# Wider warm-up matmuls, tile 2 in two token parts, and the last semaphore waits ahead of the last store

## The chip, the cores and the metric

The kernel runs on one core of a Trainium2 chip. The metric is device microseconds (us) of one execution. The kernel before takes 579.82 us as the median of 10 runs (579.07 to 580.83). A profile was taken of one execution of 579.62 us, whose span on the core is 577.9 us.

Engine names as in the profile: PE is TensorE's matmuls, PEld its weight loads, DVE is VectorE, ACT is ScalarE, POOL is GpSimd, and SP is SyncE, which here only issues DMAs and waits.

## The reference

Inputs are bfloat16; S = 2048 tokens, D = 576 features, F = 4608 hidden features, 32 heads of 18.

```python
xn = layernorm(x)                                   # no scale, no shift
q, k, v = split(xn @ wqkv)                          # 32 heads of 18
scores = q @ k.T * 18 ** -0.5                       # key at most 255 tokens back, never ahead
s = (softmax(scores) @ v) @ wo
h = sigmoid(xn @ w_gate) * (xn @ w_up)
g = silu(h @ w_down)
out = x + s * g
```

So one normalized input feeds two branches, a sliding-window attention and a gated feed-forward network, whose results are multiplied.

## The kernel before

Tokens are worked in 4 chunks of 512, each of 4 blocks of 128. For each chunk: layer norm on DVE (with a power on POOL for the reciprocal root), a transposed copy `xnT` with features on partitions, projections of v, q and k, attention for 8 groups of 4 heads, the output projection, then the feed-forward network: 36 gate/up tiles of 128 hidden features over the chunk's 512 tokens, and the down projection, accumulated over all 36 tiles for each block of tokens. A final step multiplies the branches, adds x and stores the block.

576 is 4.5 times 128. So all large matmuls come in pairs that use 64 rows of the array each and run side by side (`pair`); 5 blocks of 128 contraction rows, one of them holding the first 64 features twice, make a whole product (`turn`). A gate/up tile is 5 pairs (`f10`, first half) and 4 pairs (`f11`, second half) of 512 columns; one member of the pair writes gate, the other up. This is why layer norm writes 640 columns: the first 64 are stored a second time (`ln:dup`), for chunk 0 by POOL from x itself, for later chunks by a DVE copy of what `ln:ap` wrote.

A gate/up tile occupies one of the PSUM slots of pool F (a slot is two banks; a third slot is shared with pool S, which serves everything else). ACT takes tanh of gate (L887), DVE multiplies it with up into `hT` (L890, `hm`), and then the slot is free. A scores matmul (`sc`) occupies a slot of pool S until ACT has taken its exponential (L701).

Nothing of the order on an engine is written by hand. `build_graph` makes a list of operations with dependencies, an engine, an estimated duration, and a priority. `schedule` plays them through with those estimates: among the operations that are ready it takes the earliest, each point of priority counting as 10 ns of delay, and so fixes each engine's instruction order and the PSUM slot of each tile. `emit` writes the five instruction streams, with a semaphore wait ahead of an instruction where it needs another engine's result; each engine then runs its stream in order. A DMA has a lane, a semaphore of its own kind; there are 58 lanes.

The beginning: the four blocks of chunk 0 are loaded by one DMA each, then the weights. While layer norm works on them, PE multiplies zeros (`warm`): 60 operations, each a pair of 256 columns, estimated at 220 ns for the first 18 and 110 ns for the rest, with low priority, so that `schedule` fits them where PE would stand. When the first gate/up matmul is placed, those left over are dropped; 45 are in the stream: 24, the transposes of block 0, 12, those of block 1, 9. The first three gate/up tiles of chunk 0 are begun before all tokens are there. Each is cut into parts by token blocks (`PARTS`: block 0, block 1, blocks 2 and 3), and `build_ffn` lists part by part, first halves of the three tiles, then second halves.

The end: PE's last matmuls are the down projection of the last block. ACT and DVE make the last columns, SP stores the block. After its last DMA, SP waits on every lane in turn, at most two lanes in one instruction (L1149 to L1151), and the kernel ends when all engines have met:

```python
            if e == "SP":
                for i, n in enumerate(lane_cnt):
                    if n > 0:
                        eng.wait_ge(lanes[i], n)
                eng.nop()
```

The softmax here doesn't subtract the row's maximum and nothing guards it: scores larger than these inputs give would overflow.

## Time and profile before

| what | us |
|---|---|
| median of 10 runs | 579.82 |
| lowest and highest | 579.07, 580.83 |
| the profiled execution | 579.62 |
| its span on the core | 577.9 |
| PE busy in it | 570.5 |
| DVE, ACT, POOL busy | 345.8, 267.8, 180.0 |
| first matmul of zeros | 1.15 |
| first matmul of real data | 9.10 |
| first gate/up matmul over all 512 tokens | 15.84 |
| last DVE sum begins | 574.45 |

How to read the lines. A timeline line gives the start in us, the time from the first start to the last end in us, engine, line, operation, the tile written and the tile read, and how many instructions of the kind are merged in it; in brackets stand the engine's idle time before it and what ended that. The start-to-start distance is the time that a matmul takes of PE; the time of a single one is longer, since matmuls are pipelined. PE's matmuls are counted one by one, so a pair is x2. A line of one source line gives the count, the duration in ns as minimum, median and maximum, and the first and the last start. A line of waits gives the total in us, the number and the longest. The chain's line gives each engine's share of the chain of work that ended last.

### The profile page before, as it was taken

Reading aid. Unit: us, or ns where it says so; the run is one execution under the profiler, and the core shown is the slowest. Engines: PE = TensorE matmul, PEld = TensorE weight load, DVE = VectorE, ACT = ScalarE, POOL = GpSimd, SP = SyncE. Lnnn points to the kernel's source line nnn. Section 1 sums busy time; section 2 is a strip of 40 time slices with the busy share of each in tenths; the row PEclk is TensorE's granted clock in tenths of the full one; section 3 lists DMA queues with packets and bytes.
Section 4 is the critical chain, followed back from the end, with each engine's and each line's share of the span. In section 5 each row is a group of like instructions: output and inputs, shape, how many; then the busy total and the mean of one; then the engine's idle time right before and its main releaser. Section 6 shows DMA issues by size and latency. Waiting matters only on the chain.

```text
span 577.9 us, 21485 instructions
## 1 busy us (share of the span) xinstructions
PE 570.5 (99%) x9542; PEld 361.7 (63%) x9542; DVE 345.8 (60%) x837; ACT 267.8 (46%) x379; POOL 180.0 (31%) x290
## 2 busy tenths in 40 slices
PE   9999999999999999999999999999999999999996
PEld 7455455678985556555788875555457754444786
DVE  4478889845899775577876578877321133333123
ACT  2257567421776653866663566685221023232111
POOL 7466454107564443145534354340000000000000
PEclk9999999999999999999999999999999999999999
DMA  8978865822313434233511023343440015442010
GB/s 248 265 201 206 230 185 165 200 46 55 89 51 108 120 98 116 83 92 103 110 36 43 19 63 103 105 117 111 116 141 23 23 58 154 133 137 74 2 43 23
DMA packets 104908, 62.06 MB, mean 107 GB/s; under 512 B 15308, under 2 KB 103452, under 8 KB 104816
## 3 DMA queue, kind: packets, MB, share of 16 engines
q1 hardware_dynamic: 99696, 55.95, 35.5%
q0 software_dynamic: 5120, 4.74, 3.3%
q8 instruction: 75, 1.23, 0.9%
q14 instruction: 17, 0.14, 0.1%
HBM read 51.61 MB, written 2.36 MB: 93 GB/s over the span
## 4 chain that ended last, share of the span: by engine, by line
PE 97%; DVE 2%; issue 1%; ACT 0%; DVEq 0%
PE ps L98 96%; DVE hT L890 1%; PE ps L550 1%; ACT tring L887 0%; DVE pvs L767 0%; DVE s_attn L994 0%; DVE thf L999 0%; DVE xf L1004 0%; DVE expr L714 0%; DVE pvs L771 0%; DVE hT L418 0%; DVE small L486 0%; DVE small L409 0%; ACT expr L701 0%; DVEq L1144 0%
## 5 line engine op out<-in xcount | busy, mean ns | idle before, releaser
L98 PE MATMUL ps<-xnT,wgs 64*128 64x512 bf16 (+2 forms) x2400 | 288.3, 368 | 0.1
L98 PEld LDWEIGHTS ps<-xnT,wgs 64*128 64x128 bf16 x2400 | 111.4, 94 | 113.9 <-PE ps L98 1.6
L701 ACT ACTIVATE expr<-ps 128x1024 bf16<-128x1024 f32 (+2 forms) x160 | 156.2, 983 | 52.2 <-PE ps L98 51.7
L98 PE MATMUL ps<-wd_sb,hT 64*128 64x288 bf16 (+2 forms) x2448 | 154.9, 276 | 0.0
L887 ACT ACTIVATE tring<-ps 128x512 bf16<-128x512 f32 x144 | 85.7, 596 | 129.6 <-PE ps L98 127.1
L890 DVE SCALAR_TENSOR_TENSOR hT<-tring,ps 128x512 bf16<-128x512 bf16 x144 | 98.6, 686 | 78.5 <-ACT tring L887 76.4
L98 PEld LDWEIGHTS ps<-wd_sb,hT 64*128 64x128 bf16 x2448 | 117.8, 94 | 22.5
L254 POOL DMA_DIRECT2D qk<-qd x160 | 82.3, 522 | 85.7 <-DVE qd L588 48.0
L666 POOL TENSOR_SCALAR kx<-kprev,small 128x256 bf16<-128x256 bf16 x64 | 64.8, 1022 | 72.0 <-PE ps L98 71.6
L714 DVE TENSOR_TENSOR expr<-expr,mask 128x256 bf16<-128x256 bf16 (+2 forms) x232 | 64.9, 301 | 29.8 <-ACT expr L701 28.4
L767 DVE TENSOR_REDUCE pvs<-ps 64x304 f32<-64x608 f32 x64 | 50.4, 788 | 17.5 <-PE ps L98 16.3
L98 PE MATMUL ps<-qk,kx 64*128 64x320 bf16 (+4 forms) x736 | 59.8, 251 | 0.0
L98 PE MATMUL ps<-xnT,wgr 64*128 64x512 bf16 (+2 forms) x300 | 55.8, 368 | 1.4 <-DVE hT L890 1.2
L98 PEld LDWEIGHTS ps<-qk,kx 64*128 64x128 bf16 x736 | 31.6, 94 | 25.4 <-ACT expr L701 1.7
L984 ACT ACTIVATE thf<-ps 128x576 bf16<-128x576 f32 (+3 forms) x22 | 11.4, 519 | 70.0 <-PE ps L98 69.5
L98 PEld LDWEIGHTS ps<-v_aug,expr 64*128 64x128 bf16 x2432 | 35.5, 93 | 6.2 <-issue 0.2
L98 PE MATMUL ps<-v_aug,expr 64*128 64x19 bf16 (+1 forms) x2432 | 35.8, 170 | 0.0
L98 PE MATMUL ps<-xnT,wqk 64*128 64x512 bf16 x256 | 32.0, 376 | 0.0
L588 DVE CAST qd<-ps 128x1024 bf16<-128x1024 f32 (+1 forms) x20 | 22.1, 1115 | 7.7 <-PE ps L98 7.5
L666 DVE TENSOR_SCALAR kx<-qk,small 128x512 bf16<-128x512 bf16 x64 | 23.7, 390 | 5.1 <-DMA qk<-qd 4.4
L987 DVE SCALAR_TENSOR_TENSOR thf<-thf,ps 128x576 bf16<-128x576 bf16 x12 | 9.1, 755 | 29.3 <-ACT thf L984 28.8
L670 POOL COPY kprev<-qk 128x256 bf16<-128x256 bf16 x32 | 13.5, 430 | 33.2 <-DVE kx L666 32.7
(66 smaller groups left out, 296.1 us busy)
## 6 DMA issues: line engine op xcount, KB each, us to landing
wgs<-in_B_w_gate_dram SPq DMA_DIRECT2D x72, 256.0 KB, 3.0
wgs<-in_B_w_up_dram SPq DMA_DIRECT2D x72, 256.0 KB, 3.5
wd_sb<-in_B_w_down_dram SPq DMA_DIRECT2D x9, 576.0 KB, 4.6
qk<-qd POOLq DMA_DIRECT2D x100, 36.0 KB, 2.0
xf<-in_A_x_dram SPq DMA_DIRECT2D x16, 144.0 KB, 2.5
out_dram<-xf SPq DMA_DIRECT2D x16, 144.0 KB, 1.8
xr<-in_A_x_dram SPq DMA_DIRECT2D x6, 288.0 KB, 3.7
wqk<-in_A_wqkv_dram SPq DMA_DIRECT2D x2, 576.0 KB, 6.2
```

What stands on the lines that cost most here:

```text
L98: res = eng.matmul(outs[i], lhs(ROWS[t], i), rhs(ROWS[t], i), start=start, stop=stop, tile_position=(64 * t, 0))
L254: o = self.op(eng, DMA_ISSUE_NS[eng], lambda e: e.dma_start(dst, src), name, deps, prio, nbytes=nbytes)
L588: return eng.tensor_copy(dst, self.both(h, n))
L666: return e.tensor_scalar(self.kx[:, sx, pos:pos + n_ // SW, t, :], src.rearrange("p (s k) -> p s k", k=SW), self.half[:, t:t + 1], None, A ...
L670: self.op_kp[hg] = op("POOL", 420, lambda e: e.tensor_copy(self.kprev[:, hg, :], self.qk[:, qs, 1, NT // 2:NT]), f"kp:{c}:{hg}", deps=[kxo ...
L701: return eng.activation(self.expr[:, se, :, lo * SW:NT], self.both(h, NT)[:, :, lo * SW:NT], ACTF.Exp, scale=SM_SCALE)
L714: return eng.tensor_tensor(e_, e_, m_, ALU.mult)
L767: return eng.tensor_reduce(out[ROWS[i]], src, mybir.AxisListType.X, ALU.add)
L887: th = op("ACT", act_ns(NT), lambda e: e.activation(self.tring[:, st, :], bank(h, 0), ACTF.Tanh, scale=0.5), f"th:{c}:{ft}", deps=[pg, dt_ ...
L890: mu = op("DVE", dve_ns(NT), lambda e: e.scalar_tensor_tensor(self.hT[:, ft, :], self.tring[:, st, :], 1.0, bank(h, 1), ALU.add, ALU.mult) ...
L984: return e.activation(v2(t)[:, a:b, :], y2()[:, a:b, :], ACTF.Tanh, scale=0.25)
L987: q1 = op("DVE", dve_ns(w), lambda e: e.scalar_tensor_tensor(v2(t), v2(t), 1.0, y2(), ALU.add, ALU.mult), f"fq1:{nm}", deps=[th, f2], prio=0)
```

## The change

There are four edits.

- The warm-up matmuls become 512 columns wide; there are up to 36, estimated at 432 ns for the first 9 and 216 ns for the rest. The zeros that they read are 512 columns, so the memset is twice as large.
- `PARTS` is given for each tile: tiles 0 and 1 as before, tile 2 in two parts (blocks 0 and 1, blocks 2 and 3). The list is made tile by tile, part by part, without the order of first and second halves over the tiles; `schedule` orders them by readiness.
- For chunk 0 too, the first 64 columns are stored a second time by a DVE copy after `ln:ap`.
- SP waits on all lanes but those of the output stores ahead of its last instruction, the last store; after it, on the store lanes only.

`XPRIO` is 0, so the priority of the loads of x is what it was. Since durations, engines and parts differ, `schedule` gives other orders throughout. In the built streams there are now 25 warm-up pairs (15, the transposes of block 0, 7, those of block 1, 3), and 9 pairs fewer in the first three tiles; DVE has four copies more and POOL four operations fewer; the counts of all other matmuls, of ACT's work and of DMAs are the same. In chunk 1, the first projection of q and k and the first scores stand earlier: the scores begin after the third group of down-projection matmuls of chunk 0's second block, not after the second group of its second half. PE's order from the end of chunk 3's attention on (beside tile 21 of chunk 2's gate/up tiles) is the same.

```diff
--- before.py
+++ after.py
@@ -53,8 +53,9 @@
 NQD = 2
 NFIN = 2
 NTAIL = 96
-NWARM = 60
-PARTS = ((0, 1), (1, 2), (2, 4))
+NWARM = 36
+PARTS = (((0, 1), (1, 2), (2, 4)), ((0, 1), (1, 2), (2, 4)), ((0, 2), (2, 4)))
+XPRIO = 0
 NQK = 5
 
 DMA_ISSUE_NS = {"SP": 640.0, "POOL": 520.0, "ACT": 650.0}
@@ -379,7 +380,7 @@
     def load_x(self, c, i=0):
         if c == 0:
             for i in range(BPC):
-                self.x_dma[i] = (self.dma(self.x0[:, i, :], self.x[i * P:(i + 1) * P, :], P * D * 2, f"dma:x{i}", ("x0", i), prio=0),
+                self.x_dma[i] = (self.dma(self.x0[:, i, :], self.x[i * P:(i + 1) * P, :], P * D * 2, f"dma:x{i}", ("x0", i), prio=XPRIO * (i > 1)),
                                  self.x0[:, i, :])
             return
         st = c * BPC + i
@@ -414,7 +415,7 @@
         self.op_ident = op("POOL", 200, lambda e: e.affine_select(
             self.ident[:, :], self.ident[:, :], pattern=[[1, SW]], compare_op=ALU.not_equal, fill=1.0, base=SW,
             channel_multiplier=-1), "init:ident3", deps=[o2], prio=0)
-        zero = self.hT[:, 0, 0:2 * P]
+        zero = self.hT[:, 0, :]
         z = op("DVE", 600, lambda e: e.memset(zero, 0.0), "init:zero", prio=0)
         self.op_tab = op("ACT", 1500, lambda e: e.activation(self.tring[:, 0, 0:1], zero[:, 0:1], ACTF.Exp), "init:tab",
                          deps=[z], prio=0)
@@ -422,8 +423,8 @@
         w = None
         for i in range(NWARM):
             def f_warm(eng):
-                return pair(eng, self.halves(h, 2 * P), lambda r, t: zero[r, 0:P], lambda r, t: zero[r, :], True, True)
-            w = op("PE", 220 if i < 18 else 110, f_warm, f"warm:{i}", deps=[z], prio=4, acq=None if i else h, odeps=[w])
+                return pair(eng, self.halves(h, NT), lambda r, t: zero[r, 0:P], lambda r, t: zero[r, :], True, True)
+            w = op("PE", 432 if i < 9 else 216, f_warm, f"warm:{i}", deps=[z], prio=4, acq=None if i else h, odeps=[w])
             w.filler = h
             h.release(w)
 
@@ -493,17 +494,11 @@
             ap = op("DVE", 430, lambda e, ss=ss, x_in=x_in, sn=sn: e.tensor_scalar(
                 self.xnr[:, sn, RD:XW], x_in, self.mv[:, ss, 0:1], self.rstd[:, ss, :],
                 ALU.subtract, ALU.mult), f"ln:ap:{st}", deps=[rs, ag, dn], prio=pr)
-            if c:
-                dup = op("DVE", 180, lambda e, sn=sn: e.tensor_copy(self.xnr[:, sn, 0:RD], self.xnr[:, sn, RD:2 * RD]),
-                         f"ln:dup:{st}", deps=[ap], prio=pr)
-            else:
-                dup = op("POOL", 260, lambda e, ss=ss, x_in=x_in, sn=sn: e.tensor_scalar(
-                    self.xnr[:, sn, 0:RD], x_in[:, 0:RD], self.mv[:, ss, 0:1], self.rstd[:, ss, :],
-                    ALU.subtract, ALU.mult), f"ln:dup:{st}", deps=[rs, ag, dn], prio=pr)
+            dup = op("DVE", 180, lambda e, sn=sn: e.tensor_copy(self.xnr[:, sn, 0:RD], self.xnr[:, sn, RD:2 * RD]),
+                     f"ln:dup:{st}", deps=[ap], prio=pr)
             if c:
                 self.r_xr.release(i % 2, ap)
             self.r_st.release(ss, ap)
-            self.r_st.release(ss, dup)
             if c:
                 fl = self.flip(self.xnT[:, xs, :, i * P:(i + 1) * P], self.xnr[:, sn, :], f"flip:x:{st}", ("fx", xs, i),
                                deps=[dup, war], prio=2)
@@ -867,7 +862,7 @@
 
         def gate_up(ft, h, half, acq, part=None, deps=()):
             sw, fc = slots[ft // WG], slice((ft % WG) * P, (ft % WG + 1) * P)
-            b0, b1 = (0, BPC) if part is None else PARTS[part]
+            b0, b1 = (0, BPC) if part is None else PARTS[ft][part]
             t0, n = b0 * P, (b1 - b0) * P
             xin = self.op_xnT[c][b0:b1]
 
@@ -899,15 +894,14 @@
             weights(0)
             weights(1)
             hs = [self.pool_f.hold() for _ in range(2)] + [self.pool_s.hold()]
-            his = [None] * early
-            for part in range(len(PARTS)):
-                los = [gate_up(ft, hs[ft], 0, None if part else hs[ft], part, [his[ft]]) for ft in range(early)]
-                for ft in range(early):
-                    u = his[ft] = gate_up(ft, hs[ft], 1, None, part, [los[ft]])
-                    if part == len(PARTS) - 1:
-                        tail(ft, hs[ft], u)
-                    if part == len(PARTS) - 1 and ft == 1:
-                        self.r_w.release(slots[0], u)
+            for ft, h in enumerate(hs):
+                u = None
+                for part in range(len(PARTS[ft])):
+                    lo = gate_up(ft, h, 0, None if part else h, part, [u])
+                    u = gate_up(ft, h, 1, None, part, [lo])
+                tail(ft, h, u)
+                if ft == 1:
+                    self.r_w.release(slots[0], u)
         for ft in range(early, NFT):
             if ft % WG == 0 and ft // WG not in slots:
                 weights(ft // WG)
@@ -1001,7 +995,8 @@
             h.release(w0)
             h.release(th1)
         self.op_q2[sb] = q2
-        q3 = op("DVE", dve_ns(w, 2.0), lambda e: e.tensor_tensor(xf, xf, t, ALU.add), f"fq3:{nm}", deps=[q2, o_dx], prio=2)
+        q3 = op("DVE", dve_ns(w, 2.0), lambda e: e.tensor_tensor(xf, xf, t, ALU.add), f"fq3:{nm}",
+                deps=[q2, o_dx], prio=2)
         self.r_th.release(st, q3)
         if c0 == 0:
             self.fq3 = []
@@ -1126,12 +1121,18 @@
                     cnt[e] += 1
                     o.tok = (("E", e), cnt[e])
 
+        outs = [i for lane, i in self.lane_ids.items() if lane[0] == "out"]
+
         def semof(key):
             return lanes[key[1]] if key[0] == "L" else self.sem[key[1]]
 
         def run_engine(e, eng):
             known = {}
             for o in self.prog[e]:
+                if e == "SP" and o is self.prog[e][-1]:
+                    for i, n in enumerate(lane_cnt):
+                        if n > 0 and i not in outs:
+                            eng.wait_ge(lanes[i], n)
                 waits = {}
                 for d in o.deps:
                     k, v = d.tok
@@ -1146,9 +1147,8 @@
                 if o.needs_tok:
                     ins.then_inc(semof(o.tok[0]), 16 if o.lane is not None else 1)
             if e == "SP":
-                for i, n in enumerate(lane_cnt):
-                    if n > 0:
-                        eng.wait_ge(lanes[i], n)
+                for i in outs:
+                    eng.wait_ge(lanes[i], lane_cnt[i])
                 eng.nop()
 
         with nc.Block() as block:
```

## The prediction

> **What bounds the kernel now.** I read the page's engine table and its chain first, then the timeline of the first 17 us, then the chain's pieces and the timeline where the chain leaves TensorE, and last the sync queue's waits behind the final store.

> ```profile
> span 577.9 us, 21485 instructions
> PE 570.5 (99%) x9542; PEld 361.7 (63%) x9542; DVE 345.8 (60%) x837; ACT 267.8 (46%) x379; POOL 180.0 (31%) x290
> ...
> PE 97%; DVE 2%; issue 1%; ACT 0%; DVEq 0%
> ```

> TensorE is busy from 1.15 us to about 573 us and holds 97% of the chain. So time moves in three ways only: when the first real matmul starts, where TensorE stands still between, and what follows its last matmul. The start:

> ```profile
> 0.93 0.17 DVE L418 MEMSET hT<- 128x128 uint32 x1
> 1.15 5.30 PE L98 MATMUL ps<-hT 64*128 64x256 bf16 x48 [1.15 <-DVE hT L418]
> 6.24 0.47 PE L550 MATMUL ps<-ident,xnr 64*128 64x64 bf16 x10
> 6.53 1.61 PE L98 MATMUL ps<-hT 64*128 64x256 bf16 x24
> 8.12 1.14 PE L98 MATMUL ps<-hT 64*128 64x256 bf16 x18
> 9.10 0.22 PE L98 MATMUL ps<-xnT,wgr 64*128 64x128 bf16 x2
> 10.53 0.31 PE L550 MATMUL ps<-ident,xnr 64*128 64x64 bf16 x10
> 10.88 0.70 ACT L527 ACTIVATE xnT<-ps 128x640 bf16<-128x640 bf16 x1 [1.85 <-PE ps L550]
> 12.21 0.28 PE L98 MATMUL ps<-xnT,wgr 64*128 64x256 bf16 x2
> 15.84 0.39 PE L98 MATMUL ps<-xnT,wgr 64*128 64x512 bf16 x2
> ```

> The reader should divide. From 1.15 to 6.24 us stand 48 warm-up matmuls, 24 pairs, so 212 ns a pair of 256 columns; from 8.12 to 9.10 stand 9 pairs, 109 ns each. The array runs at half rate first; single starts put the change at about 6.8 us, 5.65 us after the first matmul, though the granted-clock row shows full speed throughout. Real work, at 9.10, begins only when the 45 warm-up pairs ahead of it in the queue are through: its weights had landed by 7.9 us and its first tokens were in SBUF at 7.46. So the warm-ups, not the data, set the start here.

> Inside, TensorE waits for a PSUM slot of the gate/up ring, which the DVE product at L890 frees:

> ```profile
> 69.94 0.39 PE L98 MATMUL ps<-xnT,wgr 64*128 64x512 bf16 x2 [0.22 <-DVE hT L890]
> 104.58 0.39 PE L98 MATMUL ps<-xnT,wgr 64*128 64x512 bf16 x2 [0.63 <-DVE hT L890]
> 259.29 0.39 PE L98 MATMUL ps<-xnT,wgr 64*128 64x512 bf16 x2 [0.20 <-DVE hT L890]
> ```

> The idle time in brackets, up to 0.63 us, ends with that product; these places hold most of what TensorE loses inside. The end:

> ```profile
> 574.45 0.26 DVE L1004 TENSOR_TENSOR xf<-xf,thf 128x192 bf16<-128x192 bf16 x1
> SPq L1151 <- DMA out_dram<-xf: 0.6, 1, 0.6
> L1151 SPq EVENT_SEMAPHORE  x15: 27/28/28, 576.5 to 577.4; - x15
> L1154 SPq COMPARE_BRANCH  x1: 41/41/41, 577.5 to 577.5; - x1
> ```

> The last store is issued at 574.73 and lands, by its median of 1.8 us, at 576.5. The sync queue has walked 13 of its waits by then, stands 0.6 us on the store's own, and then walks 15 at L1151, the store's own the first, and one at L1152: 0.97 us from 576.53 to the branch at 577.50, with the data out.

> **The change part by part.** The sum is made against the profiled execution: 579.62 us, 577.9 of it span and 1.7 around it; it lies 0.20 under the median of 579.82.

> *The tail.* All waits but those on the two store lanes now stand ahead of the last store, some 28 instructions. At (577.43 - 576.53)/15 = 0.06 us each they need 1.7 us, and the sync queue is idle there for 4.8 us (store before at 569.9, this one at 574.73), so they are free; every lane waited on had landed. After the store two waits are left. Saved: 577.50 - 576.53 = 0.97, less one remaining step of 0.06. Against it, the wait for the last DVE sum now stands in an instruction of its own, 0.06 us ahead of the store. Net -0.85 us. Ends: -0.97, and 0 if something else held the end.

> *Warm-ups.* The built order holds 25 pairs of 512 columns ahead of the first gate/up matmul, not 45 of 256: 15, the first transposes, 7, the second transposes, 3. That is 12,800 columns for 11,520, and 1,280 more at 2,400 a us are 0.53 us. The memset doubles; 0.165 us holds about 0.13 of per-column work, so TensorE begins 0.13 later, of which half, 0.07, remains if the clock opens at the same instant, since the later start costs half-rate time. Pair for pair (109 against 106.7 ns) 20 fewer save 0.04. First real matmul: 9.10 + 0.56 = 9.66. The planner counts 9 cold pairs, 3.9 us; at 5.65 us it is 13. If the clock opens sooner or later, both kernels move alike, by half the difference, so the 0.56 stays. Lower end: if wide matmuls open it sooner, a cold phase of 3.9 instead of 5.65 us takes off 0.87, which makes -0.3. Upper end: the memset's 0.13 in full and no saving on pairs, +0.7. I take 0.56, by the clock of the only row.

> [...]

> *Duplicates of the first 64 columns, POOL to DVE.* Four POOL instructions of 0.73 us (L500) go, four DVE copies of 0.175 (L497's median, 0.12 to 0.37) come. The first tile: 5.43 + 0.18 = 5.6 instead of 5.81, but its transposes now stand behind 15 wide pairs, at about 7.2. The fourth tile's apply at 9.36 had waited 0.9 us for a power on POOL that stood behind a duplicate; it comes up to 0.2 sooner in spite of 0.5 us more DVE work ahead. POOL's constants start earlier. None ends last: 0.

> *Tile order.* Tile 2 in two parts makes 9 fewer pairs at 2.3 ns: -0.02. The fourth transposes move back. From 9.66 they follow 18 pairs of 128 columns (1.00), 14 more with one set of transposes (0.92), and 5 of 256 (0.55): 12.13. Their eviction before ended 1.05 us after their start (10.53 to 11.58), so 13.2, and with the hop 13.25. TensorE gets there at 12.13 + 0.15 + 0.22 + 0.44 = 12.94: a wait of 0.3. Before, this stretch had gaps of 0.18 and 0.07, with TensorE waiting for nothing shown. Net +0.05, ends -0.25 and +0.35. Start in all: +0.6; the next full tile, before at 15.84, goes to about 16.4.

> *The middle.* The planner is run anew with the other times, and shuffles everything after 16 us: same instructions, other neighbours. I bound it from the order. A gate/up tile waits where TensorE has less work than tanh + product + hops (0.60 + 0.69 + about 0.3 = 1.6 us) between the last matmul of the tile that held the slot and its own first. Taken from the start of one pair to the next, less its columns at 2,400 a us, before lost 0.34 (tile 12) and 0.39 (tile 21), both with 1.25 us between; 0.06 (tile 32, 1.36); 0.79 (tile 34, 1.14, with a whole reduction ahead of the product), all in chunk 0; and 0.36 and 0.32 (tiles 30 and 35 of chunk 1, 1.30 each): 2.26. The new order has tiles 12, 21 and 32 as before, no such place at 34, and 1.30 at tile 20 of chunk 1 and at tiles 4 and 15 of chunk 2, say 0.34 each: 1.81. That is -0.45. One scores slot with 1.08 us between cost 0.21 and goes: -0.2. Chunk 1's attention now begins beside the last gate/up tiles and the down projection of chunk 0, where three output projections now follow their transposes within 1.0 us (five in the whole kernel within 1.1; before two, at 0.98 for nothing and at 1.08 for 0.11). DVE, which evicts those transposes, is busier there: +0.3, from 0 to 0.6. Middle -0.35; ends -1.5 (all these waits gone) and +1.5 (four more of 0.36 net).

> Sum: -0.85 + 0.6 - 0.35 = -0.6. 579.62 - 0.6 = 579.0; on the median, 579.2. I give 579.0.

> **The rivals.** *The middle gives more.* The start costs 0.3 and the middle gives 0.9, which is 1.81 us of expected waits down to 1.3: -0.85 + 0.3 - 0.9 = -1.45, 578.2. For it: chunk 1's attention moves beside down-projection matmuls, which ask neither tanh nor product. Against: chunk 0's order hardly changes.

> *Slower: the down projection no longer covers attention.* ScalarE needs five exps of 0.98 us on average (L701), 4.9 us, per head group; packed beside down projections, score slots free late and TensorE, in order, stands. Without the middle the sum is -0.25; at 0.36 us a wait, it takes four more than before to pass +1.16 (0.2%), and six give +1.9: 581.5. Against: the new order keeps 1.30 us or more between scores that share a slot in chunks 1 to 3, where before 1.36 cost nothing.

> *The tail gives nothing,* because the store lands later or the end hangs on another engine: -0.6 + 0.85 = +0.25, 579.9. Against: all other engines had drained by 574.8, and TensorE's queue by 573.3.

> **How the numbers follow.** 0.2% of 579.82 is 1.16 us, about what a measurement here can tell from no change. Forecast 0.49, the middle 0.35, slower 0.12, no tail 0.04. So faster 0.35, same 0.53, slower 0.12. The range runs from 577.6 (start +0.3, middle -1.5) to 580.6 (start +0.7, middle +1.2), which leaves about one in ten on either side.

> **What would show it.** In the changed profile: first real matmul at 9.6 to 9.8; a stand of about 0.3 near 13; the first full tile near 16.4; gate/up waits at tiles 12 and 21 of chunk 0 but not 34; after the last store two waits, and the branch within 0.15 us of its landing. It is wrong if the clock opens at another point (first real matmul below 9.2), or if the middle's losses differ from before by over 1 us.

## The result and the profile after

The changed kernel takes 578.29 us (median of 16 runs, 577.52 to 579.85) where the kernel before, run beside it, takes 580.30 (median of 55). The ratio is 0.9962, with a 95% interval from 0.9951 to 0.9973: 0.4% faster, about 2 us. The profiled execution took 577.83 us with a span of 575.8, against 579.62 and 577.9.

In the changed kernel the lines of the source stand a little elsewhere: L98, L550, L527, L890 and L1004 of before are now L99, L545, L522, L885 and L998.

The page's engine table and its chain, after:

```profile
span 575.8 us, 21364 instructions
PE 569.1 (99%) x9484; PEld 350.9 (61%) x9484; DVE 347.0 (60%) x841; ACT 268.6 (47%) x379; POOL 174.8 (30%) x286
...
PE 97%; DVE 1%; ACT 1%; issue 1%; DVEq 0%
```

TensorE still holds the chain, so the 2.1 us of span lie again in the start, in TensorE's stands inside, and in the end. The timeline of the start, after:

```profile
0.95 0.27 DVE L419 MEMSET hT<- 128x256 uint32 x1
1.28 5.15 PE L99 MATMUL ps<-hT 64*128 64x512 bf16 x30 [1.28 <-DVE hT L419]
4.98 0.96 PEld L99 LDWEIGHTS ps<-hT 64*128 64x128 bf16 x10 [0.16 <-issue]
6.42 1.67 PE L99 MATMUL ps<-hT 64*128 64x512 bf16 x14
8.07 0.81 PE L99 MATMUL ps<-hT 64*128 64x512 bf16 x6
8.72 0.22 PE L99 MATMUL ps<-xnT,wgr 64*128 64x128 bf16 x2
9.37 1.12 DVE L494 TENSOR_SCALAR xnr<-x,small 128x576 bf16<-128x576 bf16 x1 [0.23 <-POOL small L489]
9.40 0.93 POOL L451 MEMSET v_aug<- 128x192 bf16 x1
12.41 0.10 PEld L99 LDWEIGHTS ps<-xnT,wgr 64*128 64x128 bf16 x2 [0.41 <-ACT xnT L522]
12.41 0.28 PE L99 MATMUL ps<-xnT,wgr 64*128 64x256 bf16 x2
15.61 0.38 PE L99 MATMUL ps<-xnT,wgr 64*128 64x512 bf16 x2
```

The weight loads merge into one row of ten from 4.98 us on, because the pairs then follow at 0.216 us instead of 0.427: TensorE's rate doubled there, 3.70 us after the first matmul, not 5.7. Such a doubling at the start is what "the clock opened" means below; it is read from the distances, and the granted clock that the profile shows reads 1.00 on both sides of it. So real work starts at 8.72 us (9.10 before) although there are more warm-up columns. The wait for the late tokens, at 12.41, cost 0.30 us. The first full tile starts at 15.61, only 0.23 sooner than before. The rows at 9.37 and 9.40 are taken up at the end.

Inside, the same kind of timeline as before, TensorE behind the product at L885:

```profile
69.60 0.39 PE L99 MATMUL ps<-xnT,wgr 64*128 64x512 bf16 x2 [0.23 <-DVE hT L885]
234.18 0.39 PE L99 MATMUL ps<-xnT,wgr 64*128 64x512 bf16 x2 [0.25 <-DVE hT L885]
350.60 0.39 PE L99 MATMUL ps<-xnT,wgr 64*128 64x512 bf16 x2 [0.62 <-DVE hT L885]
379.97 0.39 PE L99 MATMUL ps<-xnT,wgr 64*128 64x512 bf16 x2 [0.17 <-DVE hT L885]
```

The 0.63 us of before at 104.58 is gone, and another of 0.62 has come at 350.60. What stands ahead of that one, in the timeline:

```profile
347.64 1.61 DVE L762 TENSOR_REDUCE pvs<-ps 64x304 f32<-64x608 f32 x2 [0.60 <-PE ps L99]
348.78 0.59 ACT L882 ACTIVATE tring<-ps 128x512 bf16<-128x512 f32 x1
349.77 1.28 DVE L885 SCALAR_TENSOR_TENSOR hT<-tring,ps 128x512 bf16<-128x512 bf16 x2
```

The tanh was ready at 349.37, but DVE, which had been reducing until 349.25 and then had two small operations to do, began the product only at 349.77. The end, from the timeline and the tables of the lines L1135 (the waits ahead of the last store), L1152 and L1154:

```profile
573.20 0.26 DVE L998 TENSOR_TENSOR xf<-xf,thf 128x192 bf16<-128x192 bf16 x1
573.55 0.34 SPq L255 DMA_DIRECT2D out_dram<-xf  x1
L1135 SPq EVENT_SEMAPHORE  x27: 28/28/28, 568.7 to 570.3; - x27
L1152 SPq EVENT_SEMAPHORE  x1: 17/17/17, 575.4 to 575.4; - x1
L1154 SPq COMPARE_BRANCH  x1: 41/41/41, 575.4 to 575.4; - x1
```

27 waits are walked from 568.7 to 570.3, while the sync queue has nothing else to do, and the branch follows the store's landing at once. From the start of the last DVE sum to the end of the span it is now 575.81 - 573.20 = 2.61 us, where it was 577.89 - 574.45 = 3.44.

So the two profiles differ by -0.23 us at the start, -0.84 at the end, and -0.88 in TensorE's losses after the first full tile (4.12 us before, 3.24 after: all distances between matmul starts, less their columns at the prediction's 2,400 a us, where more than 0.04 is left over; in both profiles most pairs of 512 columns follow at 0.216 us, which is 2,370 a us). That is -1.95 of the 2.08; the rest lies in smaller distances.

### The profile page after: what moved, and what is told of

The parts are those of the page before. It is cut to its first block, busy times and chain, and to the rows that moved or that the text cites. A ratio compares the mean times of both kernels' runs of the same rounds, so it can differ in the third digit from the quotient of the medians.

```text
span 575.8 us, 21364 instructions
## 1 busy us (share of the span) xinstructions
PE 569.1 (99%) x9484; PEld 350.9 (61%) x9484; DVE 347.0 (60%) x841; ACT 268.6 (47%) x379; POOL 174.8 (30%) x286
## 4 chain that ended last, share of the span: by engine, by line
PE 97%; DVE 1%; ACT 1%; issue 1%; DVEq 0%
PE ps L99 97%; DVE hT L885 1%; PE ps L545 1%; ACT tring L882 0%; DVE s_attn L988 0%; ACT expr L696 0%; DVE thf L993 0%; ACT xnT L522 0%; DVE xf L998 0%; DVE hT L419 0%; DVE small L487 0%; DVE small L410 0%; DVEq L1145 0%; DVE expr L709 0%
## 5 line engine op out<-in xcount | busy, mean ns | idle before, releaser
L99 PE MATMUL ps<-xnT,wgs 64*128 64x512 bf16 (+2 forms) x2384 | 288.3, 369 | 0.1
L99 PEld LDWEIGHTS ps<-xnT,wgs 64*128 64x128 bf16 x2384 | 110.9, 94 | 113.7 <-PE ps L99 1.4
L99 PE MATMUL ps<-wd_sb,hT 64*128 64x288 bf16 (+2 forms) x2448 | 154.4, 276 | 0.0
L885 DVE SCALAR_TENSOR_TENSOR hT<-tring,ps 128x512 bf16<-128x512 bf16 x144 | 98.6, 686 | 80.5 <-ACT tring L882 78.4
L99 PEld LDWEIGHTS ps<-wd_sb,hT 64*128 64x128 bf16 x2448 | 112.5, 94 | 27.3
L661 POOL TENSOR_SCALAR kx<-kprev,small 128x256 bf16<-128x256 bf16 x64 | 63.5, 1002 | 53.1 <-PE ps L99 52.5
L99 PE MATMUL ps<-qk,kx 64*128 64x320 bf16 (+4 forms) x736 | 59.4, 251 | 0.0
L99 PE MATMUL ps<-xnT,wgr 64*128 64x512 bf16 (+2 forms) x298 | 55.6, 369 | 1.6 <-DVE hT L885 1.3
L99 PEld LDWEIGHTS ps<-qk,kx 64*128 64x128 bf16 x736 | 31.3, 94 | 25.6 <-ACT expr L696 1.1
L99 PEld LDWEIGHTS ps<-v_aug,expr 64*128 64x128 bf16 x2432 | 35.3, 93 | 6.3 <-DVE hT L885 0.5
L99 PE MATMUL ps<-v_aug,expr 64*128 64x19 bf16 (+1 forms) x2432 | 35.8, 170 | 0.0
L99 PE MATMUL ps<-xnT,wqk 64*128 64x512 bf16 x256 | 31.9, 376 | 0.0
L643 ACT ACTIVATE v_aug<-ps 64x288 bf16<-64x288 f32 x32 | 13.1, 410 | 22.4 <-PE ps L99 21.9
```

The source lines that it names most:

```text
L99: res = eng.matmul(outs[i], lhs(ROWS[t], i), rhs(ROWS[t], i), start=start, stop=stop, tile_position=(64 * t, 0))
L643: return eng.activation(dst, src, ACTF.Copy)
L661: return e.tensor_scalar(self.kx[:, sx, pos:pos + n_ // SW, t, :], src.rearrange("p (s k) -> p s k", k=SW), self.half[:, t:t + 1], None, A ...
L885: mu = op("DVE", dve_ns(NT), lambda e: e.scalar_tensor_tensor(self.hT[:, ft, :], self.tring[:, st, :], 1.0, bank(h, 1), ALU.add, ALU.mult) ...
```

## The experiments

**The changed kernel again.** No edit.

> The changed kernel once more, unaltered, for a second look at when the clock opens. In its first profile the pair distance falls from 427 to 216 ns at about 4.8 us, 3.5 us after the first matmul; before it was 5.65 us. Theory 'width' (512-column matmuls open the clock sooner than 256-column ones): again 3.4 to 3.7 us after the first matmul. [...]

Measured: 578.04 us, ratio 0.9959 [0.9945, 0.9973]. In its profiled execution (span 576.6) the clock opened 5.10 us after the first matmul, real work started at 9.49 and the first full tile at 16.38. The same program thus started real work 0.77 us later where the clock opened 1.40 us later, while its losses inside repeat (3.24 and 3.25 us, at the same places). Here the start was close to the one predicted; in the first profile it wasn't.

**The end alone,** in the kernel before:

```
+                if e == "SP" and o is self.prog[e][-1]:
+                    for i, n in enumerate(lane_cnt):
+                        if n > 0 and i not in outs:
+                            eng.wait_ge(lanes[i], n)
 ...
-                for i, n in enumerate(lane_cnt):
-                    if n > 0:
-                        eng.wait_ge(lanes[i], n)
+                for i in outs:
+                    eng.wait_ge(lanes[i], lane_cnt[i])
```

> The kernel before with the moved waits alone; every other instruction stands where it stood. My sum says -0.85 us (ratio 0.9985): the branch within 0.15 us of the store's landing instead of 0.97 us. Rival 'the tail gives nothing': 0.0 (ratio 1.0000), because something else holds the end.

Measured: 579.56 us, ratio 0.9986 [0.9971, 1.0000], about -0.8 us of 580.31, as the rows of the end say. But its start brought something new. The clock opened early, 3.98 us after the first matmul, and real work began at 8.51; the first full tile still came only at 17.05, 1.2 us later than before. The timeline of TensorE in this kernel:

```profile
10.76 1.07 PE L98 MATMUL ps<-xnT,wgs 64*128 64x128 bf16 x31
13.30 0.21 PE L98 MATMUL ps<-xnT,wgs 64*128 64x128 bf16 x1 [1.47 <-issue]
...
17.05 0.39 PE L98 MATMUL ps<-xnT,wgr 64*128 64x512 bf16 x2
```

TensorE stands 1.5 us in the middle of a group of 32 equal matmuls, behind nothing: "issue" is the profile's word for a wait on no engine and no transfer. It is the place of the 0.18 us at 12.08 in the profile before.

**Narrow warm-ups in the changed kernel:** each wide warm-up pair as two of 256 columns, the plan unchanged.

```
-                return pair(eng, self.halves(h, NT), lambda r, t: zero[r, 0:P], lambda r, t: zero[r, :], True, True)
+                for c in (0, 2 * P):
+                    res = pair(eng, [o[:, c:c + 2 * P] for o in self.halves(h, NT)], lambda r, t: zero[r, 0:P],
+                               lambda r, t: zero[r, c:c + 2 * P], True, True)
+                return res
```

> The changed kernel, its plan and columns unaltered, with each warm-up pair of 512 columns issued as two pairs of 256. Theory 'width': the clock opens about 5.65 us after the first matmul as before, the first real matmul moves from 8.72 to about 9.7 us, and the time rises by 0.8 to 1.0 us over the changed kernel (ratio to before about 0.998). [...]

Measured: 577.86 us, ratio 0.9959 [0.9944, 0.9974], the same as the changed kernel beside it. The clock opened 3.33 us after the first matmul: narrow warm-ups do it as soon as wide ones.

**Wide warm-ups in the kernel before:** the same 45 steps, each one matmul of 512 columns instead of a pair of 256, so half the instructions for the same columns.

```
-        zero = self.hT[:, 0, 0:2 * P]
+        zero = self.hT[:, 0, :]
 ...
-            def f_warm(eng):
-                return pair(eng, self.halves(h, 2 * P), lambda r, t: zero[r, 0:P], lambda r, t: zero[r, :], True, True)
+            def f_warm(eng, t=i % 2):
+                r = ROWS[t]
+                return eng.matmul(self.halves(h, NT)[t], zero[r, 0:P], zero[r, :], start=True, stop=True, tile_position=(64 * t, 0))
```

> The kernel before, its plan unaltered, with each warm-up pair of 256 columns issued as one half of a 512-column pair (first the upper 64 rows, then the lower), so columns and order stay and only the width changes. Theory 'width': the clock opens 3.4 to 3.7 us after the first matmul, the first real matmul comes at about 8.1 instead of 9.10 us, and the time falls by 0.8 to 1.0 us (ratio 0.998). [...]

Measured: 580.54 us, ratio 1.0004 [0.9983, 1.0026]: nothing. The clock opened early, 3.39 us after the first matmul, and real work began at 8.45, yet the first full tile came at 16.29. The stand is there again, later and in another group:

```profile
12.63 1.17 PE L98 MATMUL ps<-xnT,wgs 64*128 64x256 bf16 x22
14.59 0.28 PE L98 MATMUL ps<-xnT,wgs 64*128 64x256 bf16 x2 [0.80 <-issue]
```

So the stand isn't tied to a tile, to data or to a time. Counted in TensorE's records (weight loads, matmuls, and the semaphore and drain instructions of its sequencer) it comes after the 449th in the kernel before, in the kernel with the end alone, and here too, where 90 warm-up records fewer put other work there. That gave the new theory: TensorE had run out of fetched instructions. The DMA records have a queue for these, which the page lists as "q8 instruction"; its first packet, of 16 KB, arrived at 10.67 us in the kernel before, 11.82 with the end alone and 13.30 here, and TensorE went on at 12.08, 13.30 and 14.59: 1.3 to 1.5 us after each. The page of the kernel before has, in packets, MB and the share of 16 engines' span:

```profile
q8 instruction: 75, 1.23, 0.9%
```

**Many small warm-ups,** the test of that theory: in the changed kernel the last ten planned warm-ups become eight pairs of 64 columns each, the same columns in 280 more instructions.

```
-            def f_warm(eng):
-                return pair(eng, self.halves(h, NT), lambda r, t: zero[r, 0:P], lambda r, t: zero[r, :], True, True)
+            def f_warm(eng, n=NT if i < 15 else 64):
+                for c in range(0, NT, n):
+                    res = pair(eng, [o[:, c:c + n] for o in self.halves(h, NT)], lambda r, t: zero[r, 0:P],
+                               lambda r, t: zero[r, c:c + n], True, True)
+                return res
```

> The changed kernel, plan and columns unaltered, with each of the last 10 warm-up pairs issued as 8 pairs of 64 columns: 280 more TensorE instructions between 6 and 9 us, 0.16 us more work. Theory 'fetch' (TensorE runs dry at a fixed instruction, about the 448th, and the next block comes 3.8 to 5.8 us after about the 192nd): a gap of 1 to 3 us without any semaphore in the first real matmuls, before 12 us, and a time 1 to 3 us above the changed kernel (ratio to before 0.998 to 1.001). Rival (the gap at 12 us before was a late weight or token): no such gap, time as the changed kernel plus 0.2 us (0.9965).

Measured: 583.63 us, ratio 1.0064 [1.0042, 1.0086], some 5 us slower than the changed kernel, more than the 1 to 3 us expected. TensorE's timeline in it:

```profile
9.81 0.22 PE L99 MATMUL ps<-xnT,wgr 64*128 64x128 bf16 x2
12.74 1.30 PE L99 MATMUL ps<-xnT,wgs 64*128 64x128 bf16 x24 [2.71 <-issue]
...
19.54 0.61 PE L99 MATMUL ps<-xnT,wgs 64*128 64x256 bf16 x8 [0.20 <-PE ps L99]
...
21.21 0.38 PE L99 MATMUL ps<-xnT,wgr 64*128 64x512 bf16 x2
```

The long stand comes after exactly the 449th record again, and the next, which loses 0.36 us, after the 705th, 256 later. The first two packets of the instruction queue arrived at 11.25 and 18.17 us, 1.5 and 1.4 us before TensorE went on. That bears the fetch theory out: same columns, more instructions, and the stands at the count it names. By these counts, 256 records to a packet of 16 KB, a record is 64 bytes.

The packets of all twelve profiles say the same. There are 74 or 75 places at record 449 plus a multiple of 256 in each, and as many packets, give or take one. Taken in order, the packet had arrived 1.26 to 1.59 us before TensorE went on at each of the 13 places where it stood for over 0.1 us with no wait behind it; at all others it had been there for at least 1.48 us.

The loss beyond the stands is in the clock. From 13.0 us on pairs of 128 columns follow at 107 ns instead of 55. In the profile's table of stretches (length; busy time and count of PE, PEld, DVE, ACT and POOL; the granted clock; DMA share and GB/s):

```profile
13.00:16.40 3.40, 3.40 (x68) 3.21 (x64) 0.00 (x0) 0.00 (x0) 3.24 (x3) 0.50 1.03 339
16.40:17.60 1.20, 1.10 (x32) 0.76 (x26) 0.49 (x1) 0.70 (x1) 1.20 (x2) 1.00 1.12 293
```

After the long stand TensorE was granted half its clock (0.50) for 3.4 us, which by that costs 1.7 us. With the two stands (2.9 and 0.36) that is about the delay of the first full tile: it came at 21.21 where the unaltered changed kernel, with nearly the same opening, had it at 16.38.

The count explains the small gaps deep inside as well. In the profile before, the 0.23 us at 257.39 follow record 8,897 = 449 + 33 x 256. Such places, at 449 plus a multiple of 256, also hold 0.65 us at 286.45 in the kernel before with wide warm-ups, and 0.13 us at 292.04 in the next one below. They change from execution to execution: a second profile of the kernel before has none after its start.

**Short last warm-ups:** the last ten planned, all that stand behind the first transposes, have 64 columns.

```
-            def f_warm(eng):
-                return pair(eng, self.halves(h, NT), lambda r, t: zero[r, 0:P], lambda r, t: zero[r, :], True, True)
+            def f_warm(eng, n=NT if i < 15 else 64):
+                return pair(eng, self.halves(h, n), lambda r, t: zero[r, 0:P], lambda r, t: zero[r, 0:n], True, True)
```

> The changed kernel, its plan unaltered, with the last 10 of the 25 warm-up pairs 64 columns wide instead of 512, so 4,480 columns less ahead of the first real matmul, 1.87 us at full rate. If the warm-ups in the queue set the start: the first real matmul comes at about 8.0 us (weights land at 7.9) instead of 8.7 to 9.5, the two late blocks of tokens (transposed at 10.8, copied by 11.9) become the limit, and the time falls by 0.4 to 1.2 us below the changed kernel (ratio to before about 0.9945). If the instruction fetch sets it (next block there some 3.8 to 5.8 us after the 192nd instruction): a gap within a tile at the 448th TensorE instruction, and no gain (0.996).

Measured: 577.62 us, ratio 0.9948 [0.9935, 0.9962]: the best version, clearly ahead of the kernel before; its interval overlaps the changed kernel's. TensorE's timeline:

```profile
8.20 0.23 PE L99 MATMUL ps<-xnT,wgr 64*128 64x128 bf16 x2 [0.37 <-ACT xnT L522]
...
10.82 0.28 PE L99 MATMUL ps<-xnT,wgr 64*128 64x256 bf16 x2 [0.41 <-DMA wgs<-in_B_w_up_dram]
...
15.68 0.38 PE L99 MATMUL ps<-xnT,wgr 64*128 64x512 bf16 x2
```

Real work now waits for its data, first for the tokens and at 10.82 for weights. The clock opened 5.09 us after the first matmul, and the first full tile came at 15.68; with the same opening, the unaltered changed kernel had it at 16.38. The warm-up columns behind the first transposes cost 0.7 us in such an execution.

**The same, with POOL's constants later,** so that they don't run beside the fourth token block's normalization on DVE:

```
-        d = [self.ln_rs]
+        d = [self.ln_rs, self.ln_ap]
 ...
+            self.ln_ap = ap
```

(`d` is what the memsets of `v_aug` wait for, `ap` the normalization.)

> As the run with short late warm-ups, and POOL's memset of the ones waits until DVE has normalized the fourth block. In the changed kernel that normalization took 1.12 us where the three others took 0.43, with the memset running from 0.03 us after its start. If the memset slows it: back to 0.43 us, the fourth transposes and their copies up to 0.4 us sooner, and the time 0.2 to 0.5 us below the run with short warm-ups alone. If the 1.12 us have another cause: they stay, and the times agree within 0.2 us.

Measured: 577.84 us, ratio 0.9952 [0.9940, 0.9965], no gain. The normalization itself did become short again, in DVE's timeline:

```profile
9.34 0.43 DVE L494 TENSOR_SCALAR xnr<-x,small 128x576 bf16<-128x576 bf16 x1 [0.23 <-POOL small L489]
```

It took 1.12 us in the changed kernel. The 0.7 us weren't on the path: with the slow normalization, in the run above, the fourth block's duplicate was done at 10.62, and TensorE reached its transposes only at 11.37, behind its own work; the wait for the late tokens hardly changed. This profile also has two instruction stands inside, 0.25 us at 249.22 and 0.32 at 292.32, where the run above has the one of 0.13.

**One warm-up pair less.** 24 steps in the plan instead of 36 leave 24 pairs ahead of real work instead of 25, and with them the planner gives, from the first full tile on, TensorE's order of the kernel before.

```
-NWARM = 36
+NWARM = 24
```

> The changed kernel with 24 instead of up to 36 warm-up pairs, so one less than the 25 in its stream. With that the planner gives TensorE, from the first full gate/up tile on, the very order of the kernel before. So start and tail are those of the changed kernel, less 0.2 us of warm-ups, and the middle is that of before. If the middle's order is worth what its tile waits say (4.1 us lost before, 3.2 in the changed kernel): 0.7 to 0.9 us slower than the changed kernel (ratio to before about 0.9975), with the 0.79 us wait at tile 34 back. If the middle is worth nothing: as the changed kernel (0.9955 to 0.996).

Measured: 578.88 us, ratio 0.9961 [0.9945, 0.9977]. The waits of before are back with their order, to 0.1 us: the timeline shows

```profile
104.56 0.39 PE L99 MATMUL ps<-xnT,wgr 64*128 64x512 bf16 x2 [0.63 <-DVE hT L885]
```

and the losses after the first full tile are 4.35 us, 0.48 of them a stand at 286.83 (record 449 + 37 x 256). Without that stand it is 3.87, against 3.24 in the changed kernel, and before it is 4.12 - 0.23 = 3.89. In time this can't be told from the changed kernel: the ratio is the same, since the kernel before ran at 580.71 in this comparison, while the median is 0.6 to 0.8 us above the changed kernel's. The traces give the order some 0.6 us; the times neither show it nor speak against it.

**Another shuffle,** the short last warm-ups with half the planner's weight for priorities:

```
-    PRIO_NS = 10.0
+    PRIO_NS = 5.0
```

> The changed kernel with short late warm-ups (the fastest so far, 0.9948), and the planner's weight of a priority point halved from 10 to 5 ns, which gives another order with fewer short distances: gate/up tiles 12 and 21 of chunk 0 (1.25 us), 17 of chunk 1 and 5 of chunk 2 (1.30 us), two scores slots at 1.08 us. By these distances 1.4 us of tile waits instead of 2.3: ratio to before 0.993 to 0.994. If distances in the order do not foretell the waits: no gain or a loss (0.9945 to 0.998).

Measured: 579.11 us, ratio 0.9972 [0.9961, 0.9983], some 1.5 us slower than with the plan it was taken from. The waits at gate/up tiles came where its order foretold them, 1.6 us for 1.4, but the losses after the first full tile are 5.03 us. The largest of the others: 0.37 and 0.52 us at scores slots (105.26 and 350.28), and 0.76 in four places at the output projections of chunk 0 (121.9 to 124.4).

**The kernel before again.** No edit.

> The kernel before, unaltered, for a second look at its start. Theory 'fetch': a gap within a tile at the 448th TensorE instruction, ending 1.3 to 1.5 us after the first 16 KB instruction block has arrived, and longer the sooner the clock opens; the first full tile between 15.8 and 17.1 us. If the gap belongs to a late weight: at another instruction, or none.

One execution took 579.65 us with a span of 577.9. The clock opened 5.22 us after the first matmul, 0.5 sooner than in the first profile, and real work started 0.2 sooner, at 8.90. But the packet arrived at 10.97 instead of 10.67, the stand after the 449th record cost 0.65 us instead of 0.18, and the first full tile came at 16.11, 0.27 later.

## Why the prediction was right and where it failed

The forecast was 579.0 us, 0.6 less than the profiled execution, with the larger chance on no difference that can be measured; the kernel is 2 us faster. The time was inside the range and 0.7 under the forecast, which is where the rival *the middle gives more* stood (578.2). That is partly luck. The rival had the start at +0.3, and part of its 0.9 us in the middle came from elsewhere, as shown below; and the kernel before, at 580.30 beside the changed one, lay 0.7 above the execution that the sum set out from, so of the difference itself the forecast has less than a third.

*The tail* was right: -0.85 predicted, -0.84 in the profiles, about -0.8 in the run that has it alone, whose interval reaches from nothing to -1.7.

*The start* was wrong: +0.6 predicted, -0.23 between the two profiles, and the prediction's own sign of it, a first real matmul below 9.2, came (8.72). Two things were taken wrongly. First, one row's clock opening, 5.65 us, was carried over as the value for both kernels. It differs from execution to execution: 3.33 to 5.73 us with narrow warm-ups, 3.39 to 5.10 with wide ones. The arithmetic on top of it was nearly sound: carried from 5.65 to an opening of 5.10 us, its 9.66 and 16.4 become 9.4 and 16.1, and with that opening the changed kernel started real work at 9.49 and its first full tile at 16.38.

Between the widths no difference is to be seen within that scatter, 2.4 us over all profiles, and what sets the point was not shown. The larger memset's 0.13 us was an estimate: it took 0.272 us instead of 0.165, 0.11 more, and the first matmul came at 1.28 instead of 1.15.

Second, the sentence that failed was "both kernels move alike". They don't, because the kernel before stands after record 449, by the reading above at the end of its fetched instructions. In its three profiles (the end alone has the same start) the openings were 5.73, 5.22 and 3.98 us and real work started at 9.10, 8.90 and 8.51, but the first full tile came at 15.84, 16.11 and 17.05. TensorE had used up what it had at nearly the same time in all three (the last record ahead of the stand began at 11.85, 11.64 and 11.62); the packet came at 10.67, 10.97 and 11.82, and the first full tile moved with it, to 0.1 us. So a late packet, more than the early clock, swallowed the gain. That an early clock makes the packet late is not shown: in the twelve profiles the first packet arrived 2.3 to 4.3 us after TensorE passed record 193, 256 ahead of the stand, and neither end goes with the clock (4.27 us with an opening of 3.98, but 2.28 with one of 3.33).

The changed kernel has 80 warm-up instructions fewer (20 pairs, each two loads and two matmuls) and 36 fewer in tile 2; it reaches record 449 at 14.5 us, and its packet had arrived at 11.75 (15.3 and 12.9 in its second profile). Neither of its two profiles has a stand there, so what the clock gives it keeps: its first full tile came at 15.61 with the early clock and at 16.38 with the late. With narrow warm-ups, 100 records more, it reached record 449 at 11.78; it didn't stand there either, since its packet had come early, at 9.88. So fewer instructions give the start slack, and what the slack is worth differs from execution to execution. The sign was in the profile before, in the 0.18 us that ended "with TensorE waiting for nothing shown", which the prediction counted as one of the gaps that go and did not ask for a cause.

*The wait for the late tokens,* 0.3 us predicted, was 0.30. *The duplicates on DVE* cost nothing, as predicted, though one side effect wasn't foreseen: POOL's earlier memset slowed a normalization (1.12 us instead of 0.43), which was off the path.

*The middle* had the right sign, but not by its terms: -0.35 predicted, -0.88 measured. Of that, 0.23 is an instruction stand that the second profile of the kernel before doesn't have; the order's own part is about 0.65. The places that lost more than 0.1 us after 17 us, worked out from the starts as above (three of 0.12 us at second halves of tiles are in both and left out):

| kind of place | before | after | predicted change | measured change |
|---|---|---|---|---|
| gate/up tiles, first half | 2.34 | 2.25 | -0.45 | -0.09 |
| scores slots | 0.36 | 0.16 | -0.2 | -0.2 |
| output and value projections | 0.23 | none | +0.3 | -0.23 |
| inside a tile (257.39, 398.28) | 0.46 | none | not seen | -0.46 |
| attention product at 99.43 | none | 0.17 | not seen | +0.17 |

The scores slot was right. At the gate/up tiles the places were right, and one was mis-sized: tile 4 of chunk 2 (at 350.60) cost 0.78 us instead of 0.34, as much as the one at 104.58 that went. The prediction had priced that one, tile 34, with "a whole reduction ahead of the product", and did not see that the same two reductions on DVE (1.61 us from 347.64) stand ahead of the product here. The waits feared at the output projections did not come. One of the two stands inside a tile comes after record 8,897, where TensorE went on 1.3 us after the packet's arrival at 256.12, and so belongs to the instruction fetch; the one at 398.28 stands at no such record, and its cause stays open. It comes back with the old order (398.56, in the kernel with one pair less), so it belongs to the order.

*The slower rival* got no support in this order; the run with other priorities shows that its mechanism exists, since another shuffle of the same work lost 1.8 us more inside, most of it at scores slots, where TensorE waited for ScalarE's exponential, and at output projections. That *the tail gives nothing* is refuted by the profile.

What remains open is how the 2.0 us divide on average. The tail has 0.8 to 0.9 and the order, by the profiles, about 0.65. The remaining half microsecond is start and instruction stands, which differ from execution to execution; the shares are read from single profiles, and the runs are too close together to confirm them one by one.

## What to carry to other kernels

A stand of TensorE inside a group of equal matmuls that the profile puts down to "issue" should be counted in instructions before it is put aside: if such stands lie 256 records apart, many small instructions early in the kernel can cost far more than their columns, 5 us for 280 of them here. It is no rule that fewer always gain: half the warm-up instructions in the kernel before gained nothing that the times show, and 100 more in the changed kernel cost nothing; in their profiles the packet came late in the one (13.30 us) and early in the other (9.88). A start that depends on the clock's opening, 3.33 to 5.73 us after the first matmul here, is to be given as a range from several executions, for each kernel by itself, because what lies behind may swallow the gain in one and not in the other. Waits on transfers that have long landed belong ahead of the last store, where the queue is idle: here 27 of them were walked from 568.7 to 570.3 us, 3.2 us ahead of the store, and the end got 0.84 us shorter.
